# Attention feeding a routed MoE: other q and k loads and transposes, a separate load for the last queries' sums, expert weights loaded during attention

## The chip, the cores and the metric

One Trainium2 chip, one of its cores. The metric is the device time of one execution of the whole program in microseconds (us), the median of several executions. All profile times below are of one profiled execution.

## The reference, cut to what matters

The program chains three blocks on B=4 batches, H=8 heads, S=576 tokens, head size D=64 (N = 2304 tokens of width 512), all in float32:

```python
scores = scale * np.matmul(q, k.transpose(0, 1, 3, 2))          # attention, causal,
cum = np.cumsum(np.log(np.clip(f, 0.0001, 1.0)), axis=-1)       # with a decay from the forget gates f
scores = np.where(causal, -1e9, scores + cum[..., :, None] - cum[..., None, :])
attn = softmax(scores); x = matmul(attn, v)                     # -> (2304, 512)

e = argmax(x @ w_gate)                                          # MoE: 8 experts, top 1
y[mask_e] = gate_e * (relu(x[mask_e] @ w1[e]) @ w2[e])          # w1 512x1024, w2 1024x512

out = (silu(y @ w_gate2) * (y @ w_val)) @ w_out                 # GLU, width 1536
```

## The kernel before, in words

**Attention.** Work goes by pairs of heads: 16 pairs, four to a batch. A pair has five chunks of queries, `ic` 0 to 3 with 128 queries and (ic+1)·128 keys, and `ic` 4, the last 64 queries of both heads against all 576 keys, stacked into one 128-row product. For each pair:

- `load_qk` (L322) loads q and k with four DMAs each. Each partition gets 18 whole rows of 64 numbers (4608 bytes in a piece), and the two halves of a row go to two groups of 32 partitions by loading the rows twice, shifted. `qk_t` (L358) then turns 32x32 blocks on VectorE, writing with a step of 18 elements and reading 32 of every 64.
- `load_bc` (L335) broadcasts the pair's two rows of the running sums `cum` (scaled by -8) to all partitions, 576 columns a head, into the tile `bc`.
- On GpSimd, `dec_c` (L413) copies `bc` into `dec`, each head on its 64 partitions, in two copies, and adds the causal mask `future` to the last 64 columns. `qk_z` (L407) copies the last 64 queries into a block-diagonal tile `qz`, in two copies. `bc_m` (L423) writes the causal mask into each 128-column block of `bc`, once per chunk and head, after the chunk to its right has been used.
- `sc_mm` (L430) makes the scores in PSUM tiles of the tag `s` (4 buffers, two for each `ic`). `sc_max` and `sc_max4` (L451, L461) on VectorE add `bc` or `dec` and take the row's extreme. `sc_exp` (L471) exponentiates on ScalarE, `tr_mm` (L479) transposes on TensorE, `tr_ev` copies back, `av_mm` (L534) multiplies by v, `tok_mm` (L552) turns the result back to tokens and forms the gate's logits.

After each batch's last pair the routing runs: `route_a` to `route_g` on VectorE, `route_m` (L669) scales the rows of a chunk (on GpSimd for the first three batches, by the list `LAST_M` for the last), `route_w` (L687) scatters them by an indirect DMA on GpSimd to their expert's rows in DRAM, `xs`.

**What sets the order.** No engine reorders. `Plan` (L55) is a list scheduler that runs when the program is built: every step is added with an engine, a cost in ns, a priority (`PR`, plus the pair's number), dependences, buffers taken and released (`NB`), and for loads a DMA time. It simulates the engines and emits each engine's instructions in the order it finds. Where a cost or a DMA time in the plan is off, an instruction that waits stands in front of others on its engine. SyncE's DMA queue (SPq) carries all plain loads in that order.

**Pair 0** is loaded in another layout and transposed on TensorE (`first_load` to `first_e`), and its `bc` is made by a matmul from the sums in SBUF, not by a DMA (`bc_mm`, `bc_ev`).

**Bridge and MoE.** After the plan, the attention's memory is released. The pools `ring` (weights: four `raw` tiles, four `hl` tiles) and `mp` are opened on that memory. `w_load` (L908) loads a quarter of an expert's w1 (four DMAs of 128 KB) and of its w2 (one of 512 KB). At L1237 two quarters are loaded, `x_load(0)` loads expert 0's rows from `xs`, `w_split` (L926) splits the first quarter into a rounded part (ScalarE) and its remainder (VectorE), `offsets` (L1085) works out where each expert's tokens start, 24 (`NKEEP`) matmuls on constants keep TensorE going (L1245), then `x_turn` and `x_low` transpose and split the rows and `gemm1` begins. The MoE loop then runs over 8 experts with 8 chunks each. The GLU follows.

Of the kernel before, what the change touches and what calls it, by code (L numbers as in the profile page):

```python
# [20 lines left out]
P = 128  # L21
NEG = -8.0e9

PR = dict(
    ldq=-2.3,
# [5 lines left out]
    z=-0.6,  # L31
# [16 lines left out]
    zr=1.2,  # L48

# [89 lines left out]
def moe_kernel(ctx: ExitStack, tc: tile.TileContext, q, k, v, f, wgate, w1, w2, m2g, m2v, m2o, out):  # L139
# [56 lines left out]

    attn = ctx.enter_context(ExitStack())
# [25 lines left out]
    def pairwise(name, shape, fill=0.0):  # L223
        t = [one.tile(shape, F32, name=f"{name}{i}") for i in range(2)]
        return t

    v_sb = pairwise("v_sb", [P, NC, 2, D])
# [4 lines left out]
    p3 = pairwise("p3", [P, 2, 64])  # L232
    for i in range(2):
        nc.gpsimd.memset(qz[i], 0.0)
        nc.gpsimd.memset(v_sb[i][64:, NC - 1], 0.0)
# [78 lines left out]
    def load_v(p):  # L314
        b, hp = divmod(p, NP)
        for hh in range(2):
            nc.sync.dma_start(
                out=v_sb[p % 2][:, 0:4, hh], in_=v[b, 2 * hp + hh, 0:512].rearrange("(c p) d -> p c d", p=P)
            )
        nc.sync.dma_start(out=v_sb[p % 2][:64, 4], in_=v[b, 2 * hp : 2 * hp + 2, 512:576].rearrange("h p d -> p h d"))  # L320

    def load_qk(p, i):  # L322
# [3 lines left out]
        for hh in range(2):  # L326
            for dh in range(2):
                a = hh * 64 + dh * 32
                c = 32 - 32 * dh
                nc.sync.dma_start(  # L330
                    out=o.qk[i][a : a + 32, c : c + 18 * 64],
                    in_=(q, k)[i][b, 2 * hp + hh].rearrange("(c t) d -> c (t d)", t=18),
                )

    def load_bc(p):  # L335
        b, hp = divmod(p, NP)
        o = pairs[p]
# [1097 lines left out]
```

## Time and profile before

| | us |
|---|---|
| median of 3 runs | 978.03 |
| lowest, highest | 976.2, 982.95 |
| the profiled execution's own time | 977.45 |
| its span, first to last instruction | 975.7 |

| stage | from, to (us) | what ends it |
|---|---|---|
| attention, 16 pairs | 0 to 243 | last route steps |
| bridge | 243 to 266 | first `gemm1` matmul |
| MoE | 266 to 510 | |
| GLU | 510 to 976 | |

TensorE is busy for 903.8 us of the span (93%), VectorE 590.3, ScalarE 400.5, GpSimd 311.2. Engines are called PE, DVE, ACT and POOL in the rows; PEld is TensorE's weight load, SPq SyncE's DMA queue. A busy PE counts modelled ends of pipelined matmuls. "Idle before" a row, in brackets, is the time for which the engine stood idle, with what ended it. [...]

### The profile page before, as it was taken

To read this page: it belongs to the slowest core of one execution; us is meant where nothing else is said; L and a number is where in the kernel's file an instruction comes from. 1 tells how busy PE (TensorE), PEld (TensorE's weight loads), DVE (VectorE), ACT (ScalarE), POOL (GpSimd) and SP (SyncE) were. 2 spreads that over 40 slices of the span, in tenths; PEclk is the share of its full clock that TensorE was granted. 3 is DMA by queue.
4 is the path that set the end of the run, shared out by engine and by line. 5 is a ranking of instruction groups with operands and counts; after the bars stand their busy time and mean duration, and the time that the engine had idled before them with its cause. 6 is when DMAs were issued, how large, how long until landed. Compare 5 with 4: busy or idle time off the path is not lost. (4 is left out here: it accounts for less than half of the span.)

```text
span 975.7 us, 15236 instructions
## 1 busy us (share of the span) xinstructions
PE 903.8 (93%) x5046; PEld 739.0 (76%) x5048; DVE 590.3 (61%) x1409; ACT 400.5 (41%) x964; POOL 311.2 (32%) x435
## 2 busy tenths in 40 slices
PE   8988798998486999999979999999999999999995
PEld 4655455655286999999977888888888888888884
DVE  5666565675443666777872355755755756747653
ACT  5666466766333455555642522222322222222210
POOL 5335327361253000000112423423433334334334
PEclk8999899999687999999998999999999999999998
DMA  8965565620699977777632101201101111110013
GB/s 192 245 165 163 147 159 162 163 94 13 191 123 116 216 206 193 189 210 213 199 102 73 65 22 44 65 23 44 65 22 43 47 41 44 44 44 22 1 65 129
DMA packets 98562, 106.47 MB, mean 109 GB/s; under 512 B 29424, under 2 KB 80624, under 8 KB 98480
## 3 DMA queue, kind: packets, MB, share of 16 engines
q1 hardware_dynamic: 94864, 96.00, 38.9%
q0 software_dynamic: 3616, 9.46, 2.8%
q8 instruction: 41, 0.67, 0.3%
q14 instruction: 41, 0.34, 0.1%
HBM read 89.62 MB, written 15.81 MB: 108 GB/s over the span
## 5 line engine op out<-in xcount | busy, mean ns | idle before, releaser
L994 PE MATMUL h<-xhl,hl 128*128 128x320 f32 (+6 forms) x768 | 127.7, 317 | 24.0 <-ACT hl L934 12.1
L1361 PE MATMUL r<-hl,phl 128*128 128x512 f32 x594 | 146.4, 393 | 0.1
L994 PEld LDWEIGHTS h<-xhl,hl 128*128 128x128 f32 x768 | 118.2, 197 | 26.4 <-ACT hl L934 12.9
L1334 PE MATMUL v<-yh,hl 128*128 128x512 f32 (+1 forms) x440 | 134.8, 372 | 0.0
L1334 PE MATMUL g<-yh,hl 128*128 128x512 f32 (+1 forms) x440 | 134.3, 371 | 0.0
L1344 DVE TENSOR_TENSOR sg<-v,sg 128x512 f32<-128x512 f32 (+1 forms) x60 | 38.2, 636 | 158.7 <-PE v L1334 158.7
L1361 PEld LDWEIGHTS r<-hl,phl 128*128 128x128 f32 x594 | 110.8, 188 | 24.8 <-DVE acc L1366 0.5
L1366 DVE TENSOR_TENSOR acc<-r,acc 128x512 f32<-128x512 f32 x198 | 127.1, 683 | 3.9 <-PE r L1361 3.7
L1204 POOL TENSOR_TENSOR cs<-ca,cs 128x512 f32<-128x512 f32 x36 | 47.2, 1311 | 248.5 <-PE y L1013 146.2
L1349 POOL TENSOR_TENSOR phl<-sg,phl 128x512 fp32r<-128x512 f32 (+1 forms) x55 | 68.5, 1245 | 168.3 <-ACT phl L1346 168.3
L1013 PE MATMUL y<-hh,hl 128*128 128x320 f32 (+6 forms) x768 | 121.9, 309 | 0.0
L1013 PEld LDWEIGHTS y<-hh,hl 128*128 128x128 f32 x768 | 114.8, 192 | 0.0
L935 DVE TENSOR_TENSOR hl<-raw,hl 128x512 fp32r<-128x512 f32 x128 | 84.9, 708 | 42.0 <-ACT hl L934 33.1
L474 ACT ACTIVATE u<-u,mn 128x576 f32<-128x576 f32 (+2 forms) x144 | 83.7, 583 | 57.9 <-DVE mn L466 28.8
L1346 ACT ACTIVATE phl<-sg 128x512 fp32r<-128x512 f32 (+1 forms) x60 | 35.4, 591 | 166.8 <-DVE sg L1344 166.8
L456 DVE CUSTOM_DVE_ANT_0 u<-s,bc 128x512 f32<-128x512 f32 (+3 forms) x128 | 59.2, 486 | 64.2 <-PE s L444 30.3
L1334 PEld LDWEIGHTS g<-yh,hl 128*128 128x128 f32 x440 | 80.4, 188 | 15.3
L1334 PEld LDWEIGHTS v<-yh,hl 128*128 128x128 f32 x440 | 80.4, 188 | 15.1
L1343 ACT ACTIVATE sg<-g 128x512 f32<-128x512 f32 (+1 forms) x60 | 33.3, 555 | 140.9 <-PE g L1334 139.5
L934 ACT ACTIVATE hl<-raw 128x512 fp32r<-128x512 f32 x128 | 72.6, 621 | 37.8 <-DMA raw<-in_moe_w_dram 37.8
L1334 PE MATMUL v<-yl,hl 128*128 128x512 f32 (+1 forms) x220 | 81.2, 369 | 0.0
L1334 PE MATMUL g<-yl,hl 128*128 128x512 f32 (+1 forms) x220 | 81.2, 369 | 0.0
(193 smaller groups left out, 1317.9 us busy)
## 6 DMA issues: line engine op xcount, KB each, us to landing
raw<-in_moe_w_dram SPq DMA_DIRECT2D x128, 128.0 KB, 3.8
raw<-in_moe_w_dram SPq DMA_DIRECT2D x32, 512.0 KB, 4.5
qk<-in_q_dram SPq DMA_DIRECT2D x60, 144.0 KB, 4.3
qk<-in_k_dram SPq DMA_DIRECT2D x60, 144.0 KB, 5.1
bc<-cum_d SPq DMA_DIRECT2D x15, 576.0 KB, 6.2
xs<-zrow SPq DMA_DIRECT2D x8, 768.0 KB, 5.9
raw<-in_moe_w_gate_dram SPq DMA_DIRECT2D x12, 512.0 KB, 3.6
raw<-in_moe_w_val_dram SPq DMA_DIRECT2D x12, 512.0 KB, 3.5
```

What stands on the lines that cost most here:

```text
L456: nc.vector.tensor_tensor_reduce(out=st.U[:, :W], in0=st.ps[:, :W], in1=o.bc[:, hh, :W], op0=ALU.add, op1=ALU.min, scale=-0.125, scalar=3. ...
L474: nc.scalar.activation(out=st.U[:, :W], in_=st.U[:, :W], func=AF.Exp, bias=o.mn[:, x : x + 1], scale=-1.0, accum_out=o.sm[:, u : u + 1],)
L934: nc.scalar.activation(out=t[:, 0, j], in_=src[:, j], func=AF.Copy)
L935: nc.vector.tensor_tensor(out=t[:, 1, j], in0=src[:, j], in1=t[:, 0, j].bitcast(F32), op=ALU.subtract)
L994: nc.tensor.matmul(ps[:, :n], lhsT=w[:, a, c, f0 : f0 + P], rhs=xhl[e][:, b, c, :n], start=m == 0, stop=m == 3 * KC - 1)
L1013: nc.tensor.matmul(ys[e][c][:, : win(e)], lhsT=w[:, a, fc % 2, c * P : (c + 1) * P], rhs=t[:, b], start=fc == 0 and m == 0, stop=fc == NF ...
L1204: nc.gpsimd.tensor_tensor(out=s.bitcast(F32), in0=a.bitcast(F32), in1=s.bitcast(F32), op=ALU.add)
L1334: nc.tensor.matmul(pgv[fc, ti][y][:, :n], lhsT=w[:, a, y, c, :], rhs=(yh, yl)[b][:, c, t0 : t0 + n], start=m == 0, stop=m == 3 * KC - 1,)
L1344: nc.vector.tensor_tensor(out=sg[:, :n], in0=pv[:, :n], in1=sg[:, :n], op=ALU.mult)
L1349: en.tensor_tensor(out=t[:, 1, :n], in0=sg[:, :n], in1=t[:, 0, :n].bitcast(F32), op=ALU.subtract)
L1361: nc.tensor.matmul(ps, lhsT=t[:, a, x : x + P], rhs=w[:, b, :DM], start=m == 0, stop=m == 2)
L1366: nc.vector.tensor_tensor(out=o, in0=ps, in1=o, op=ALU.add)
```

## The change

- **q and k.** The loads take row t·32+c to partition c and cut each row into its two halves of 32 numbers: no byte is loaded twice, and each piece is 128 bytes. The transposes read and write whole rows of 576 without steps.
- **Sums.** `bc` covers only the first 512 columns. `dec` is loaded by two DMAs of its own (64 partitions each, 576 columns, three buffers); the two GpSimd copies are gone, and `dec_m` only adds the mask. For pair 0 `dec` comes from matmuls too.
- **Last queries.** `qz` is made by one multiplication with a 0/1 mask `own`, and waits for q's transpose alone.
- **Scores.** `ic` 0 shares the two PSUM tiles of `ic` 1.
- **Buffers and plan.** v gets three buffers; costs in the plan are changed; in the last batch the scatters no longer have an order among themselves in the plan, and `LAST_M` gives ScalarE one chunk in place of two.
- **Weights.** `ring` and a small pool `early` (for `offsets`) are opened before the attention's pools. The first two `w_load` and the first `w_split` become steps of the plan.
- `NKEEP` goes from 24 to 48.

```diff
 PR = dict(
+    ldd=-1.8,
...
+    w=0.0,
+    ws=0.0,
...
+    late = ctx.enter_context(ExitStack())
+    ring = late.enter_context(tc.tile_pool(name="ring", bufs=1))
+    early = late.enter_context(tc.tile_pool(name="early", bufs=1))
     attn = ctx.enter_context(ExitStack())
...
-    LAST_M = ["dve", "act", "dve", "act", "pool"]
-    NKEEP = 24
-    NB = dict(qk0=2, qk1=2, bc=3, qkt=2, dec=2, u=6, pt=2, s=4, t=2, o=2, v=2, x=2, xo=1, z=2)
+    LAST_M = ["dve", "dve", "act", "dve", "pool"]
+    NKEEP = 48
+    NB = dict(qk0=2, qk1=2, bc=3, qkt=2, dec=3, u=6, pt=2, s=4, t=2, o=2, v=3, x=2, xo=1, z=2)
...
                 nc.sync.dma_start(
-                    out=o.qk[i][a : a + 32, c : c + 18 * 64],
-                    in_=(q, k)[i][b, 2 * hp + hh].rearrange("(c t) d -> c (t d)", t=18),
+                    out=o.qk[i][a : a + 32, :S].rearrange("p (t d) -> p t d", d=32),
+                    in_=(q, k)[i][b, 2 * hp + hh].rearrange("(t c) d -> c t d", c=32)[:, :, dh * 32 : dh * 32 + 32],
                 )
...
-        nc.sync.dma_start(out=o.bc, in_=cum_d[None, h : h + 2, :].to_broadcast([P, 2, S]))
+        nc.sync.dma_start(out=o.bc, in_=cum_d[None, h : h + 2, :512].to_broadcast([P, 2, 512]))
+
+    def load_dec(p):
...
+        for x in range(2):
+            nc.sync.dma_start(
+                out=o.dec[x * 64 : x * 64 + 64], in_=cum_d[None, h + x, :].to_broadcast([64, S])
+            )
...
-        nc.vector.transpose(
-            out=o.t[:, i].rearrange("p (c t) -> p t c", t=18),
-            in_=o.qk[i][:, 32:].rearrange("p (t x) -> p t x", x=64)[:, :, 0:32],
-        )
+        nc.vector.transpose(out=o.t[:, i], in_=o.qk[i][:, :S])
...
-        for hh in range(2):
-            r = slice(hh * 64, hh * 64 + 64)
-            pcopy(qz[p % 2][r, hh * 64 : hh * 64 + 64], pairs[p].t[r, 0, 512:576])
+        nc.gpsimd.tensor_tensor(
+            out=qz[p % 2].rearrange("p (h i) -> p h i", h=2), in0=own,
+            in1=pairs[p].t[:, 0, None, 512:576].to_broadcast([P, 2, 64]), op=ALU.mult,
+        )
...
-        for hh in range(2):
-            r = slice(hh * 64, hh * 64 + 64)
-            pcopy(o.dec[r], o.bc[r, hh])
-        d = o.dec[:, 512:576]
+        d = pairs[p].dec[:, 512:576]
         nc.gpsimd.tensor_tensor(out=d, in0=d, in1=future, op=ALU.add)
...
+        for c, at in ((0, 256), (1, 0)) if ic == 1 else ((ic, 0),):
+            W = (c + 1) * P
...
-            lb = add("sp", 475, p + PR["bc"], partial(load_bc, p), [fs], acq=["bc"], data=1900)
+            lb = add("sp", 475, p + PR["bc"], partial(load_bc, p), [fs], acq=["bc"], data=1500)
+            ldc = add("sp", 900, p + PR["ldd"], partial(load_dec, p), [fs], acq=["dec"], data=800)
...
-        z = add("pool", 500, p + PR["z"], partial(qk_z, p), tt, acq=["z"])
-        dc = add("pool", 1560, p + PR["dc"], partial(dec_c, p), [lb], acq=["dec"])
+        z = add("pool", 420, p + PR["z"], partial(qk_z, p), tt[:1] if p else tt[4:5], acq=["z"])
+        dc = add("pool", 280, p + PR["dc"], partial(dec_m, p), [ldc])
...
-            c = 2 * c_f32(W) if ic == 4 else 1.5 * c_f32(W) + 200
+                c = {4: 1020, 3: 1060, 2: 840, 1: 960}[ic]
...
-                t = add("pe", (ic + 1) * 109, kk + PR["tr"] + 0.001 * hh, partial(tr_mm, p, hh, ic, st), [e], acq=["t"],
+                t = add("pe", (ic + 1) * 110 + 90, kk + PR["tr"] + 0.001 * hh, partial(tr_mm, p, hh, ic, st), [e], acq=["t"],
...
+    for qi in range(2):
+        l = add("sp", 2250, NPR - 3 + PR["w"] + qi, partial(w_load, 0, qi), data=4500)
+        if qi == 0:
+            d = l
+            for part in range(2):
+                for x in range(2):
+                    d = add("act", c_act(512), NPR - 1 + PR["ws"] + 0.1 * (2 * part + x), partial(w_hi, 0, 0, part, x), [l, d])
+                    d = add("dve", c_dve(512), NPR - 1 + PR["ws"] + 0.1 * (2 * part + x), partial(w_lo, 0, 0, part, x), [d])
     plan.run()
...
-    w_load(*qs[0])
-    w_load(*qs[1])
     x_load(0, 0)
-    w_split(0, 0, 0)
-    w_split(0, 0, 1)
     places = offsets()
```

## Rows read from the trace of the kernel before

**Rows 1.** Busy time by stage: PE, PEld, DVE, ACT, POOL, clock, DMA share, GB/s.
```profile
15.00:243.00 228.00, 201.73 (x1344) 128.00 (x1345) 144.37 (x542) 148.90 (x469) 95.70 (x230) 0.96 0.58 151
243.00:266.00 23.00, 8.37 (x29) 3.52 (x30) 10.48 (x55) 7.52 (x24) 5.96 (x6) 0.69 0.64 174
266.00:317.00 51.00, 38.86 (x201) 37.41 (x201) 21.60 (x47) 15.44 (x33) 20.68 (x20) 0.77 1.00 127
317.00:510.00 193.00, 190.28 (x1337) 189.56 (x1336) 139.81 (x298) 104.03 (x225) 8.41 (x6) 1.00 0.71 191
510.00:975.00 465.00, 451.79 (x2088) 373.75 (x2088) 266.83 (x429) 118.20 (x206) 172.10 (x140) 0.99 0.15 48
```

**Rows 2.** Line L466, the first DVE step of each pair: ns min/median/max, first to last start.
```profile
L466 DVE CUSTOM_DVE_ANT_0 u<-s,dec x16: 395/444/457, 14.5 to 223.1; 128x288 f32<-128x288 f32 x16
```

**Rows 3.** Timeline at 48 to 52 us: start, length, instruction, idle before it.
```profile
48.09 1.41 POOL L249 TENSOR_SCALAR dec<-bc 64x576 f32<-64x576 f32 x2 [5.14 <-DMA bc<-cum_d]
...
50.18 0.42 DVE L456 CUSTOM_DVE_ANT_0 u<-s,bc 128x256 f32<-128x256 f32 x1 [4.49 <-POOL bc L426]
...
51.84 0.55 PE L489 MATMUL pt<-ident,u 128*128 128x128 f32 x3 [2.60 <-ACT p L500]
```

**Rows 4.** Timeline at 103 and at 167 to 171 us.
```profile
103.63 0.24 POOL L249 TENSOR_SCALAR qz<-qkt 64x64 f32<-64x64 f32 x1 [4.73 <-DMA xs<-xo,slot_i]
103.93 2.29 PE L436 MATMUL s<-qkt,qz 128*128 128x288 f32 x4 [4.07 <-POOL qz L249]
...
167.28 0.67 POOL L249 TENSOR_SCALAR dec<-bc 64x576 f32<-64x576 f32 x1 [2.06 <-DMA xs<-xo,slot_i]
...
170.29 0.90 PE L489 MATMUL pt<-ident,u 128*128 128x128 f32 x3 [2.89 <-ACT p L500]
```

**Rows 5.** Busy time in two stretches of attention, columns as in rows 1.
```profile
100.00:120.00 20.00, 15.90 (x87) 9.08 (x89) 10.66 (x38) 9.74 (x31) 6.50 (x19) 0.83 0.40 121
160.00:180.00 20.00, 16.28 (x102) 10.26 (x101) 9.96 (x36) 12.46 (x37) 10.65 (x27) 0.91 0.66 175
```

**Rows 6.** Two DVE transposes: line L362 in attention, and L963 in the bridge's timeline.
```profile
L362 DVE STREAM_TRANSPOSE qkt<-qk x30: 1209/1252/1260, 13.4 to 210.8; 128x576 f32<-128x576 f32 x30
...
264.46 1.69 DVE L963 STREAM_TRANSPOSE xt<-xw 128x320 f32<-128x320 f32 x4 [2.17 <-DMA xw<-xs]
```

**Rows 7.** Groups by line, 0 to 260 us: count, busy us, mean ns, idle before.
```profile
L249 POOL TENSOR_SCALAR dec<-bc 64x576 f32<-64x576 f32 x32 | 21.3, 667 | 43.2 <-DMA bc<-cum_d 27.9 <-DVE mn L466 11.0 <-DMA xs<-xo,slot_i 2.1
```

**Rows 8.** DMA packets, MB and engine share in 6:7, 221:225 and 11:12 us.
```profile
q1 hardware_dynamic: 323, 0.01, 17.3%
...
q1 hardware_dynamic: 1200, 0.30, 32.5%
...
q1 hardware_dynamic: 87, 0.27, 106.5%
```

**Rows 9.** The bridge: timeline, and the five last scatters' time to landing.
```profile
247.53 1.82 SPq L913 DMA_DIRECT2D raw<-in_moe_w_dram  x4
...
250.44 0.98 POOL L690 DMA_INDIRECT xs<-xo,slot_i  x1 [0.30 <-issue]
...
DMA to landing us min/median/max: 2.8/3.3/8.8
...
259.28 1.82 SPq L949 DMA_DIRECT2D xw<-xs  x4
...
265.57 5.16 PE L994 MATMUL h<-xhl,hl 128*128 128x320 f32 x24 [11.30 <-issue]
```

**Rows 10.** The bridge: constant matmuls on PE, one weight split on ACT.
```profile
247.16 7.11 PE L1246 MATMUL y<-warm,ones 128*128 128x512 bf16 x22 [0.22 <-issue]
...
253.03 1.15 ACT L934 ACTIVATE hl<-raw 128x512 fp32r<-128x512 f32 x2 [5.57 <-DMA raw<-in_moe_w_dram]
```

**Rows 11.** Line L466 in DVE's timeline: the quickest pair.
```profile
116.74 0.43 DVE L466 CUSTOM_DVE_ANT_0 u<-s,dec 128x288 f32<-128x288 f32 x1
128.66 0.45 DVE L466 CUSTOM_DVE_ANT_0 u<-s,dec 128x288 f32<-128x288 f32 x1
```

More of the change, by code (lines that the diff above doesn't have):

```diff
@@ L221, in moe_kernel, with pairwise @@
     setup = []
[L223 to L227, printed above, removed]
+    def pairwise(name, shape, n=2):
+        return [one.tile(shape, F32, name=f"{name}{i}") for i in range(n)]
+    v_sb = pairwise("v_sb", [P, NC, 2, D], 3)
     xl = pairwise("xl", [P, NC, H, W2])
@@ L232, in moe_kernel @@
     p3 = pairwise("p3", [P, 2, 64])
+    setup_t = one.tile([B * H, 2, S], F32, name="setup_t")
+    own = one.tile([P, 2, 64], F32, name="own")
+    nc.gpsimd.memset(own, 0.0)
+    for x in range(2):
+        nc.gpsimd.memset(own[x * 64 : x * 64 + 64, x], 1.0)
+    for i in range(3):
+        nc.gpsimd.memset(v_sb[i][64:, NC - 1], 0.0)
     for i in range(2):
-        nc.gpsimd.memset(qz[i], 0.0)
-        nc.gpsimd.memset(v_sb[i][64:, NC - 1], 0.0)
         nc.gpsimd.memset(p3[i][64:], 0.0)
@@ L696, in route_w, with raw_tile, hl_tile, w_load @@
         scatters.append(i.ins)
+    def raw_tile():
+        return ring.tile([P, 1024], F32, tag="raw", name="raw", bufs=4)
+    def hl_tile():
+        return ring.tile([P, 2, 1024], F32R, tag="hl", name="hl", bufs=4)
+    raws = {}
+    def w_load(e, qi, at=None):
+        w1e, w2e = (w1[e], w2[e]) if at is None else (w1[bass.ds(at, 1)][0], w2[bass.ds(at, 1)][0])
+        a = raw_tile()
+        for blk in range(4):
+            nc.sync.dma_start(
+                out=a.rearrange("p (k f) -> p k f", k=KC)[blk * 32 : blk * 32 + 32],
+                in_=w1e[blk * P : (blk + 1) * P, qi * 256 : (qi + 1) * 256].rearrange("(k r) f -> r k f", r=32),
+            )
+        b = raw_tile()
+        nc.sync.dma_start(
+            out=b.rearrange("p (g d) -> p g d", g=2),
+            in_=w2e[qi * 256 : (qi + 1) * 256, :].rearrange("(g p) d -> p g d", p=P),
+        )
+        raws[e, qi] = (a, b)
+    hls = {}
+    def w_hi(e, qi, part, x):
+        if x == 0:
+            hls.setdefault((e, qi), []).append(hl_tile())
+        j = slice(x * 512, x * 512 + 512)
+        nc.scalar.activation(out=hls[e, qi][part][:, 0, j], in_=raws[e, qi][part][:, j], func=AF.Copy)
+    def w_lo(e, qi, part, x):
+        j = slice(x * 512, x * 512 + 512)
+        t = hls[e, qi][part]
+        nc.vector.tensor_tensor(
+            out=t[:, 1, j], in0=raws[e, qi][part][:, j], in1=t[:, 0, j].bitcast(F32), op=ALU.subtract
+        )
+    def w_split(e, qi, part):
+        for x in range(2):
+            w_hi(e, qi, part, x)
+            w_lo(e, qi, part, x)
     class St:
@@ L816, in moe_kernel @@
             mk = [
-                add("pool", 244, kk + PR["mk"], partial(bc_m, p, ic, hh), [lb, dc] + [mxs[hh, c] for c in range(ic + 1, 4)])
+                add("pool", 260, kk + PR["mk"], partial(bc_m, p, ic, hh), [lb] + [mxs[hh, c] for c in range(ic + 1, 4)])
                 for hh in range(2)
```

147 lines of the change are left out of this document (67 added, 80 removed).

## The prediction

> **What bounds the kernel now.** I read the busy time by stage first. The reader is to see there that the GLU and the MoE from 317 us on keep PE busy for 97 to 99% of the time at full clock [rows 1]: a step made earlier ahead of them can only shift them. The change works in the two stages before. Attention takes 228 us with PE busy for 88% of it, DVE 63%, ACT 65%, POOL 42%, and the DMA engines for 58%. The bridge, 23 us, leaves PE idle for nearly two thirds. Between them and the steady MoE lies a stretch, 266 to 317 us, where the DMA engines are full (1.00) and PE waits for weights.
>
> In attention the first DVE steps of the pairs spread over 208.6 us, so 15 intervals of 13.9 us [rows 2]. The timeline shows what lengthens some of them. At 48 us POOL stands 5.14 us at the copy into `dec` for the next pair, because that pair's `bc` has not landed; the masks of the current pair stand behind it, DVE waits 4.49 us, and PE loses 2.60 us [rows 3]. Twice POOL stands until a scatter has landed: at 103 us the second half of `qz` is behind it and PE loses 4.07 us, at 167 us a `dec` copy and again masks, and PE loses 2.89 us [rows 4]. The clock falls with these: the 20 us around the former were granted 0.83, around the latter 0.91 [rows 5]. As a clock of 0.5 for t takes t/2 of work away, that is 20 x 0.17 = 3.4 us and 20 x 0.09 = 1.8 us more.
>
> In the bridge the chain is: the last scatter is issued on POOL at 250.44; four of the five scatters land after some 3 us, but the slowest takes 8.8, and `x_load`, which must wait for all, goes out at 259.28, right when that one is down; 6.3 us later comes the first `gemm1` matmul [rows 9]. The weight loads, issued from 247.53 on, share the DMA engines with that scatter.
>
> **The change part by part.**
>
> *Bridge.* With two quarters (2 x 1 MB) loaded during attention, the five scatters are alone on the DMA engines. The last then lands after 2.8 to 3.3 us rather than 8.8 [rows 9]: 5.5 to 6.0 us less. `LAST_M` takes a chunk off ACT and lets POOL issue in the order in which chunks come ready, worth 0 to 1 us; I take none. But PE must also get through 48 constant matmuls before `gemm1`: 22 took 7.11 us and ended at 254.27 [rows 10], part of them at half clock; 24 more at the same 0.32 us each would be 7.8 us, at half that 3.9, so they end at 258.2 to 262.1; without them `gemm1` could start at 265.57 - 5.7 = 259.9. So the cost is 0 to 2.2 us, and near 0 as the clock has risen by then. The gain is 5.9, between 3.5 and 7. A higher clock in the first `gemm1` helps little: behind it the stretch to 317 us runs at the pace of the DMA engines [rows 1], and its loads are queued behind `x_load` as before, so that stretch is moved whole. The GLU too.
>
> *Splits in attention.* The first quarter's split is four ACT and four DVE steps: 1.15 us for two on ACT, so 2.3 us, and about as much on DVE, now in the last pair's plan, in front of steps that end the attention. ACT is idle 35% of the time, so it costs 0 to 2.3 us; I take 1. The wait for the weights is new on ACT: behind it stand the last pair's exponentials, but the ten DMAs are planned two pairs earlier. Their issue takes SPq some 5 us (1.82 us for four [rows 9]) ahead of the last v loads; a pair of 13.9 us covers that, and without the cover the last `av_mm` would wait as long.
>
> *POOL.* The two copies go, 2 x 0.667 us a pair [rows 7], and with them the place where POOL stands for `bc`. What comes in their stead is `dec_m`, which waits for its own DMA; behind it stand the masks again. But `dec` has three buffers, each free once the pair's first step has used it, so its load can be two pairs ahead. Of the three stalls I count back: 2.60 wholly; at 103 us half of 4.07 + 3.4, and at 167 us half of 2.89 + 1.8, since scatters still stand in POOL's queue. That is 2.6 + 3.7 + 2.3 = 8.6 us, between 0 (each stall moves to the next instruction in POOL's queue) and 14.8 (all go). `qz` as one step for two of 0.24 us [rows 4] changes little; that it no longer waits for k's transpose is in the same sum.
>
> *Transposes.* One takes 1.25 us for 576 columns. The nearest row without a step on the written side is the one in the bridge: four of 320 columns in 1.69 us, 0.42 each or 1.32 ns a column [rows 6]. That gives 0.76 for 576, 0.49 less, and 30 x 0.49 = 14.7 us of DVE time. DVE is not the bound (63%), but what stands behind a transpose on DVE feeds ACT and PE; the share that reaches the end lies between 0 and all. I take a third, 5 us, since PE, the busiest engine, was idle only 12%. [...]
>
> *DMA.* A 32-byte packet takes 0.173 x 16 us / 323 = 8.6 ns of one DMA engine (the window holds nearly nothing but `sel`), one of 256 bytes (v) 0.325 x 64 us / 1200 = 17.3 ns, one of 4608 bytes 1.065 x 16 us / 87, nearly 200 ns at the least as smaller ones are among the 87 [rows 8]. Before, q and k of a pair are 256 packets of 4608 bytes; by the 0.27 MB of that window in 17.0 us, 15.9 bytes a ns, they take 290 ns each and 256 x 290 / 16 = 4.6 us. After, they are 8 x 576 = 4608 packets of 128 bytes, between 8.6 and 17.3 ns each, so 2.5 to 5.0 us; on a line between the two, 12.3 ns and 3.5 us. `bc` and `dec` grow from 590 to 819 KB, at the same rate 2.3 to 3.2 us; v stays at 1152 x 17.3 / 16 = 1.2. In sum 7.9 us a pair for 8.1, of 13.9: no gain, no loss.
>
> *The rest.* Shared score tiles free two of ten takings of the four `s` buffers, v's third buffer takes waits off SPq, and more matmuls for pair 0's `dec` lengthen the start while two POOL copies there go. None has a row that prices it; with the new order as a whole I bound it by one stall of the size in rows 4 either way, -4 to +4 us, and take 0.
>
> **Sum.** 5.9 - 1 + 8.6 + 5 = 18.5 us. The profiled execution took 977.45, 1.75 over its span and 0.6 below the median, so 959.0. Extremes of the terms taken together: 3.5 - 2.3 + 0 + 0 - 4 = 2.8 us worse than before, and 7 + 14.8 + 14.7 + 4 = 40.5 better.
>
> **Rivals.**
>
> 1. *Only the bridge counts.* The stalls move to the next instruction behind the same scatters, and DVE's relief is hidden under PE at 88%. For it: two of three stalls end with a scatter [rows 4], and that is not changed. Against it: one of them is a wait for `bc` in a copy that no longer exists [rows 3]. Time: 977.45 - 5.9 + 1 = 972.5.
>
> 2. *PE becomes the pace of every pair.* The quickest pair took 11.92 us from first step to first step [rows 11]. If better costs in the plan and fewer waits brought all intervals to 12.2, attention would give 15 x 1.7 = 25.5 us, and the total is 977.45 - 25.5 - 5.9 + 1 = 947. Against it: routing steps come on top every fourth pair.
>
> 3. *Slower: small packets.* If a 128-byte packet cost 40 ns, q and k would need 4608 x 40 / 16 = 11.5 us and the pair 15.9, 2.0 more than 13.9. Over 15 pairs that is 30 us; less the bridge's 5.9 and plus 1, the time is 1003. It decides from (13.9 - 4.4) x 16 / 4608 = 33 ns on. Against it stand 17.3 ns for 256 bytes [rows 8]. [...]
>
> 4. *The loads are not ahead.* If the plan puts `w_load` so late that the weights meet the scatters again, the bridge stays and attention alone gives 13.6: 977.45 - 12.6 = 965.
>
> **How the numbers follow.** Forecast 0.62, at 959 with its own range of 951 to 967; rival 1, 0.16; rival 2, 0.12; rival 3, 0.04; rival 4, 0.06. A measurement of this kernel tells about 1%, 9.8 us, from no change: faster is below 968.2. The forecast, rivals 2 and 4 lie there, 0.80, and a quarter of rival 1's surroundings, 0.04: 0.84. Within 1% remains 0.12, slower 0.04. The range of 8 in 10 goes from 943, which takes in rival 2, to 972.
>
> **What would show it right or wrong.** In the changed profile the transposes should take about 0.8 us; no DMA of weights should be issued between attention and `x_load`; the last scatter should land after about 3 us, and `gemm1` start some 9.5 us after that scatter's issue rather than 15.1 [rows 9]; first steps of pairs should be about 13.0 us apart; POOL should have no `dec` copies, and fewer PE gaps of over 2 us should be left. The forecast is wrong if 128-byte packets take over 33 ns, if PE still has gaps of 3 us behind POOL, if the intervals fall to 12.2, or if the constant matmuls end after the rows have come.

## The result and the profile after

The changed kernel took 953.37 us, the median of 4 runs (950.29 to 959.41), beside 977.12 of the kernel before: a ratio of 0.976, with a 95% interval of 0.972 to 0.980. Measured a second time, beside the kernel before again, it had 964.22 against 982.24, 0.985 with 0.979 to 0.991. Both lie in the predicted range and on either side of the 959.0 forecast. The profiled execution is the quickest of the first four, 950.29 for 977.45 before, so its 27.2 us are more than the typical gain.

The busy time by stage of the changed kernel comes first: attention, bridge, the stretch of expert 0, the other experts, the GLU (columns as in [rows 1]; the clock is the granted share of TensorE's full one).

```profile
16.00:232.00 216.00, 196.80 (x1357) 125.34 (x1357) 140.37 (x559) 153.58 (x481) 77.91 (x188) 0.97 0.68 144
232.00:246.00 14.00, 13.40 (x51) 5.49 (x51) 6.21 (x39) 0.89 (x3) 4.16 (x4) 0.80 0.46 134
246.00:285.00 39.00, 30.97 (x180) 29.00 (x179) 17.89 (x41) 12.73 (x27) 20.55 (x20) 0.87 0.93 145
285.00:487.00 202.00, 194.41 (x1359) 192.87 (x1358) 143.21 (x305) 108.32 (x230) 8.38 (x6) 0.99 0.75 192
487.00:948.00 461.00, 451.07 (x2088) 372.74 (x2087) 266.90 (x429) 117.04 (x205) 172.34 (x140) 0.99 0.14 46
```

Beside [rows 1] the reader sees the bridge shrink from 23 to 14 us. The two stretches behind it have other borders there (266 to 317 and 317 to 510 us), so they are compared by exact borders. These are the starts of single instructions in the timelines: the matmul of `carry` that ends the attention, the `x_load` of expert 0, the first `gemm1` matmul, the first `gemm1` of expert 1, the first GLU matmul. All kernels are read by them, one profile each, in us:

| kernel | median | ratio to before (95%) | attention ends | `x_load` | first `gemm1` | expert 0 takes | expert 1 to GLU |
|---|---|---|---|---|---|---|---|
| before | 977.12 | | 246.33 | +12.95 | +6.29 | 45.7 | 202.2 |
| changed | 953.37 | 0.976 (0.972–0.980) | 232.44 | +6.83 | +6.37 | 39.4 | 201.7 |
| changed, again | 964.22 | 0.985 (0.979–0.991) | 236.06 | +6.82 | +6.23 | 46.5 | 202.3 |
| e1 weights back | 963.13 | 0.982 (0.977–0.988) | 228.82 | +10.77 | +8.18 | 45.9 | 203.8 |
| e2 24 constant matmuls | 963.79 | 0.984 (0.979–0.989) | 236.45 | +6.81 | +6.43 | 41.6 | 204.2 |
| e3 old q and k | 970.55 | 0.989 (0.982–0.996) | 240.72 | +6.82 | +6.34 | 48.9 | 202.6 |
| e4 mask order | 948.98 | 0.970 (0.965–0.975) | 217.63 | +6.90 | +6.18 | 49.0 | 204.5 |
| e5 weights late | 962.61 | 0.982 (0.977–0.987) | 230.01 | +6.85 | +6.15 | 46.4 | 204.8 |
| e6 POOL copies | 967.45 | 0.988 (0.983–0.994) | 238.61 | +6.82 | +6.29 | 45.5 | 205.3 |
| e7 old costs | 971.30 | 0.989 (0.985–0.993) | 241.45 | +6.90 | +6.30 | 49.1 | 205.7 |
| e8 order, late | 951.26 | 0.968 (0.963–0.972) | 223.27 | +6.85 | +6.23 | 54.2 | 201.6 |
| e9 perm late | 966.44 | 0.983 (0.979–0.987) | 236.61 | +6.82 | +6.33 | 28.2 | 225.6 |
| e10 order, perm | 951.71 | 0.969 (0.965–0.973) | 220.41 | +6.89 | +6.20 | 27.8 | 226.9 |
| e11 all three | 954.98 | 0.971 (0.967–0.975) | 220.89 | +6.85 | +6.28 | 31.0 | 227.4 |

Kernels measured side by side are e1 to e4, the repeat with e5 to e7, and e8 to e11; totals are compared within these groups. In the first and the last, e2 and e9 stand for the changed kernel, as their attention has its schedule. The totals expected of e1 to e4 were reckoned from 953.37, some 10 us below what the same schedule took there (963.79 in e2), so the differences count.

Of the 27.2 us between the two profiled executions, 13.9 come from the attention, 6.1 from the end of attention to `x_load`, 6.3 from expert 0 and 0.9 from the rest. The 6.3 are no effect of the change: the repeat took 46.5 us there, and over the ten kernels that leave that stretch as it was the time goes from 39.4 to 54.2. Attention spreads less: the changed one's schedule ran in four kernels (changed, its repeat, e2, e9) and ended at 232.44 to 236.61, mean 235.4. Against the one profile of before, a typical gain is 10.9 in attention and 6.1 in the bridge, 17 us of 977, which is between the two measured ratios.

The bridge, in the timeline of the changed kernel (answers to [rows 9, 10]):

```profile
232.44 0.17 PE L1147 MATMUL h<-carry,ones 128*128 128x8 bf16 x1 [1.06 <-DVE carry L672]
...
232.47 13.01 PE L1293 MATMUL y<-warm,ones 128*128 128x512 bf16 x48
...
236.09 0.98 POOL L714 DMA_INDIRECT xs<-xo,slot_i  x1 [0.30 <-DVE rk_m L1179]
...
239.27 1.84 SPq L1000 DMA_DIRECT2D xw<-xs  x4
...
245.63 4.38 PE L1045 MATMUL h<-xhl,hl 128*128 128x320 f32 x24 [0.16 <-ACT xhl L1019]
```

`x_load` goes out 3.2 us after the last scatter's issue (8.8 before), and `gemm1` starts 9.5 us after it (15.1 before). The 48 constant matmuls end at 245.48, 0.15 us ahead of `gemm1`, which waits for ACT and not for them. (The rows had landed by 244.52, when DVE began to transpose them.)

In attention the two PE gaps behind scatters have gone. The one behind `bc` at 50 us is larger, and a second one behind `bc` has come at 107 us. PE's gaps of over 2 us up to the last pair's end, 2.60, 4.07 and 2.89 before, are 4.35 and 5.41 now, 9.8 us for 9.6. The timeline of the changed kernel (answers to [rows 3, 4]):

```profile
44.08 0.45 SPq L347 DMA_DIRECT2D bc<-cum_d  x1
...
48.51 1.03 POOL L445 TENSOR_SCALAR_AFFINE_SELECT bc<-bc 128x128 f32<-128x128 f32 x4 [6.74 <-DMA bc<-cum_d]
49.33 0.29 DVE L480 CUSTOM_DVE_ANT_0 u<-s,bc 128x128 f32<-128x128 f32 x1 [4.83 <-POOL bc L445]
...
50.69 0.90 PE L513 MATMUL pt<-ident,u 128*128 128x128 f32 x3 [4.35 <-ACT p L524]
...
103.69 0.54 POOL L445 TENSOR_SCALAR_AFFINE_SELECT bc<-bc 128x128 f32<-128x128 f32 x2 [5.15 <-DMA bc<-cum_d]
105.90 0.29 DVE L480 CUSTOM_DVE_ANT_0 u<-s,bc 128x128 f32<-128x128 f32 x1 [5.91 <-POOL bc L445]
...
107.27 0.90 PE L513 MATMUL pt<-ident,u 128*128 128x128 f32 x3 [5.41 <-ACT p L524]
```

POOL now stands at a mask itself. In the order that the plan made, it is the first mask of pair 4, whose `bc` was issued on SPq at 44.08 and has landed when the mask starts at 48.51. Behind it stand the last two masks of pair 2, which is still in hand: pair 3 begins on DVE only at 50.43. What these two depend on, DVE's steps on the chunk to their right, had ended at 43.80, and yet they run only after the mask in front. DVE waits 4.83 us for one of these masks, then ACT and PE. At 103.69 it is the first mask of pair 8, ahead of the last two of pair 6. So the step in front belongs not to the next pair but to the one after it. The granted clock of the two stretches shows what follows the gaps:

```profile
41.00:61.00 20.00, 15.65 (x95) 9.68 (x95) 8.20 (x32) 10.33 (x34) 3.79 (x13) 0.83 0.94 199
98.00:118.00 20.00, 14.59 (x94) 8.80 (x92) 8.33 (x33) 10.35 (x33) 4.29 (x17) 0.83 0.71 140
50.70:57.50 6.80, 6.80 (x27) 3.23 (x29) 3.42 (x14) 3.56 (x11) 0.86 (x3) 0.56 0.92 202
```

In the 6.8 us behind the first gap (the third line) PE is busy all the time at a mean of 0.56 of its clock, so it does up to 3 us (6.8 x 0.44) less work than at full clock. In the 5.3 us ahead of the gap, from 41 to 46.3, the clock was 1.00.

By groups of the whole kernel (ns min/median/max, first to last start), the transposes fell from 1252 to 774 ns, and the first DVE steps of the 16 pairs are 12.95 us apart, (209.5 - 15.2) / 15, for 13.9 before [rows 2, 6]:

```profile
L388 DVE STREAM_TRANSPOSE qkt<-qk x30: 729/774/779, 13.4 to 193.4; 128x576 f32<-128x576 f32 x30
...
L490 DVE CUSTOM_DVE_ANT_0 u<-s,dec x16: 420/454/458, 15.2 to 209.5; 128x288 f32<-128x288 f32 x16
```

The packets of one us in which only k loads were issued, from the DMA view of 11.5 to 12.5 us:

```profile
q1 hardware_dynamic: 1098, 0.14, 85.0%
```

That is 0.85 x 16 us / 1098 = 12.4 ns for one packet of 128 bytes (0.14 MB in 1098). And one thing is far from where the prediction had it: the early weights. SPq, ACT and DVE in the timeline of 51 to 75 us:

```profile
51.99 2.01 SPq L735 DMA_DIRECT2D raw<-in_moe_w_dram  x4
54.05 0.43 SPq L740 DMA_DIRECT2D raw<-in_moe_w_dram  x1
64.28 0.63 ACT L752 ACTIVATE hl<-raw 128x512 fp32r<-128x512 f32 x1
...
66.27 2.02 SPq L735 DMA_DIRECT2D raw<-in_moe_w_dram  x4
```

Both quarters are loaded and the first split in pairs 3 to 5, not in the last pairs: in the plan these loads depend on nothing, so they go out as soon as SPq has no step of higher priority ready.

### The profile page after: what moved, and what is told of

Its sections match the earlier page's. It is cut to its first block, busy times and chain, and to the rows that moved or that the text cites. A ratio compares the mean times of both kernels' runs of the same rounds, so it can differ in the third digit from the quotient of the medians.

```text
span 948.5 us, 15310 instructions
## 1 busy us (share of the span) xinstructions
PE 901.1 (95%) x5080; PEld 733.2 (77%) x5080; DVE 581.8 (61%) x1410; ACT 399.7 (42%) x958; POOL 291.1 (31%) x389
## 5 line engine op out<-in xcount | busy, mean ns | idle before, releaser
L1045 PE MATMUL h<-xhl,hl 128*128 128x320 f32 (+6 forms) x768 | 123.5, 309 | 8.6 <-issue 6.8
L1045 PEld LDWEIGHTS h<-xhl,hl 128*128 128x128 f32 x768 | 113.8, 190 | 11.4 <-issue 7.6
L498 ACT ACTIVATE u<-u,mn 128x384 f32<-128x384 f32 (+4 forms) x144 | 83.8, 584 | 45.6 <-DVE mn L480 33.4
L480 DVE CUSTOM_DVE_ANT_0 u<-s,bc 128x128 f32<-128x128 f32 (+3 forms) x128 | 59.8, 484 | 55.0 <-POOL bc L445 28.8
L1381 PEld LDWEIGHTS v<-yh,hl 128*128 128x128 f32 x440 | 80.3, 188 | 15.1
```

The costliest lines, as they stand in the source:

```text
L480: nc.vector.tensor_tensor_reduce(out=st.U[:, :W], in0=st.ps[:, at : at + W], in1=o.bc[:, hh, :W], op0=ALU.add, op1=ALU.min, scale=-0.125, ...
L498: nc.scalar.activation(out=st.U[:, :W], in_=st.U[:, :W], func=AF.Exp, bias=o.mn[:, x : x + 1], scale=-1.0, accum_out=o.sm[:, u : u + 1],)
L1045: nc.tensor.matmul(ps[:, :n], lhsT=w[:, a, c, f0 : f0 + P], rhs=xhl[e][:, b, c, :n], start=m == 0, stop=m == 3 * KC - 1)
L1381: nc.tensor.matmul(pgv[fc, ti][y][:, :n], lhsT=w[:, a, y, c, :], rhs=(yh, yl)[b][:, c, t0 : t0 + n], start=m == 0, stop=m == 3 * KC - 1,)
```

## The experiments

**The weights taken out of attention (e1).** All weights are loaded after the attention again, as before the change; the rest of the change stays.

```diff
-    for qi in range(2):
-        l = add("sp", 2250, NPR - 3 + PR["w"] + qi, partial(w_load, 0, qi), data=4500)
-        ...
+    w_load(*qs[0])
+    w_load(*qs[1])
     x_load(0, 0)
+    w_split(0, 0, 0)
+    w_split(0, 0, 1)
```

> The changed kernel with its weight part undone: ring opened after attention, the first two quarters loaded and the first split made in the bridge, as before (the 48 constant matmuls stay). My theory, that this part is worth 5.9 us in the bridge and costs 1 in attention: about 958, with the last scatter landing after some 8 us again and x_load some 13 us after the last carry step rather than 7. Rival A, that the quicker first expert (39.4 us after the change, 45.7 before) also comes from this part: 961 to 965. Rival B, that the weight loads, which the plan issued at 52 and 66 us into full DMA queues, hold attention up: it ends earlier, and the total is 955 or less.

The bridge's timeline in e1:

```profile
232.47 0.98 POOL L711 DMA_INDIRECT xs<-xo,slot_i  x1 [0.30 <-issue]
232.62 3.07 SPq L732 DMA_DIRECT2D raw<-in_moe_w_dram  x4
...
239.59 1.82 SPq L991 DMA_DIRECT2D xw<-xs  x4
...
247.77 5.67 PE L1036 MATMUL h<-xhl,hl 128*128 128x320 f32 x24 [7.09 <-issue]
```

From the last scatter's issue to `x_load` are 7.1 us (8.8 before the change, 3.2 with the weights ahead), and from there to `gemm1` 8.2 for 6.4. Together 5.8 us of the bridge hang on the early weights, the size predicted, though a third of it (1.8) lies behind `x_load` and not in the scatter. Attention, however, ends at 228.82, some 6 us before the mean of the changed kernel: of PE's two gaps the one at 50 us is still there (3.98 us), the one at 107 us is not. What the bridge gains by the early loads, attention gives back; in the total e1 can't be told from the changed kernel.

**Fewer constant matmuls (e2).** `NKEEP` is 24 again.

```diff
-    NKEEP = 48
+    NKEEP = 24
```

> The changed kernel with 24 constant matmuls instead of 48. My theory: the clock falls before gemm1, its first 24 matmuls take some 1 us longer, and that is hidden because the stretch behind it waits for weights: 953, within 2 us. Rival: the kept clock is what made the first expert quicker (39.4 us for 45.7): 956 to 960, and the stretch from gemm1 to the second expert is back at some 45 us. Rival 2: the 48 ended after the rows had come (245.5 us), so fewer of them start gemm1 earlier: 952.

```profile
237.29 6.28 PE L1293 MATMUL y<-warm,ones 128*128 128x512 bf16 x22 [0.22 <-issue]
...
249.69 5.59 PE L1045 MATMUL h<-xhl,hl 128*128 128x320 f32 x24 [6.12 <-ACT xhl L1019]
```

In e2's bridge PE stands 6.12 us before `gemm1`, and the first 24 matmuls take 5.59 us for 4.38: 1.2 us in the place itself. Of that nothing is seen in the total (0.984, between the two measurements of the changed kernel). So the doubled count costs nothing, and what it is worth is below what can be told.

**The old loads and transposes of q and k (e3).** `load_qk` and `qk_t` as before the change, with `WQ` of 1184.

```diff
-                    out=o.qk[i][a : a + 32, :S].rearrange("p (t d) -> p t d", d=32),
-                    in_=(q, k)[i][b, 2 * hp + hh].rearrange("(t c) d -> c t d", c=32)[:, :, dh * 32 : dh * 32 + 32],
+                    out=o.qk[i][a : a + 32, 32 - 32 * dh : 32 - 32 * dh + 18 * 64],
+                    in_=(q, k)[i][b, 2 * hp + hh].rearrange("(c t) d -> c (t d)", t=18),
...
-        nc.vector.transpose(out=o.t[:, i], in_=o.qk[i][:, :S])
+        nc.vector.transpose(
+            out=o.t[:, i].rearrange("p (c t) -> p t c", t=18),
+            in_=o.qk[i][:, 32:].rearrange("p (t x) -> p t x", x=64)[:, :, 0:32],
+        )
```

> The changed kernel with the old loads of q and k and the stepped transposes; plan costs and so the order of every engine are unchanged. A transpose goes from 0.77 to 1.25 us. My theory, that a third of the VectorE time comes through: 14.4 / 3 = 5 us, so about 958. Rival A, VectorE is hidden: 953 within 2. Rival B, all of it comes through: 967. Rival C, the small packets cost more than the transposes win: under 951.

The group of transposes in e3, from the lines of 0 to 260 us (busy us, mean ns):

```profile
L388 DVE STREAM_TRANSPOSE qkt<-qk 128x576 f32<-128x576 f32 x30 | 36.7, 1251 | 3.8 <-DMA qk<-in_q_dram 2.7 <-DMA qk<-in_k_dram 0.9 <-PE s L469 0.2
```

DVE has 14 us more of transposes, and attention ends at 240.72, 5.3 later than the changed kernel's mean (4.1 to 8.3 by its single readings). That is about the third that the prediction took. The total is 6.8 us over e2's beside it, though their intervals overlap. The order of every engine is the changed kernel's here, but loads and transposes are undone together, so the price is that of both.

**The order of masks and `dec` (e4).** POOL's step on the next pair's `dec` and the next pair's masks are made to depend, in the plan, on the current pair's last masks. POOL then does the current pair's masks first. The same steps are computed. As the plan works out all queues anew, the others change as well: 53 of POOL's 196 steps stand in another order, 26 of PE's 325, 29 of DVE's 364, 26 of ACT's 325 and 2 of SPq's 88.

```diff
+    mk = []
...
-        dc = add("pool", 280, p + PR["dc"], partial(dec_m, p), [ldc])
+        dc = add("pool", 280, p + PR["dc"], partial(dec_m, p), [ldc] + mk)
+        last_mk = mk
...
-                add("pool", 260, kk + PR["mk"], partial(bc_m, p, ic, hh), [lb] + [mxs[hh, c] for c in range(ic + 1, 4)])
+                add("pool", 260, kk + PR["mk"], partial(bc_m, p, ic, hh), [lb] + last_mk + [mxs[hh, c] for c in range(ic + 1, 4)])
```

> The changed kernel with two added dependences in the plan: the first masks of a pair and the mask of dec come after the last masks of the pair before, so that nothing that waits for a pair's loads stands on GpSimd in front of the pair before. My theory, that the two TensorE gaps left (4.35 and 5.41 us, each with 6.8 us at half clock behind it, 16.6 us in all) come from that order: both gone, and 8 to 14 us less, 939 to 945. Rival: bc is late in any case, so the wait moves to VectorE's first step on bc and the time stays within 3 of 953.

POOL's largest wait in e4's attention (us in total, times, longest), the pairs' first steps, and the busy time in the two stretches:

```profile
POOL bc L445 <- DVE mn L480: 102.1, 68, 6.0
```

```profile
L490 DVE CUSTOM_DVE_ANT_0 u<-s,dec x16: 396/458/459, 14.5 to 193.8; 128x288 f32<-128x288 f32 x16
```

```profile
41.00:61.00 20.00, 19.92 (x136) 12.57 (x136) 13.49 (x53) 16.95 (x55) 4.97 (x18) 1.00 0.97 203
98.00:118.00 20.00, 20.00 (x153) 13.53 (x153) 13.12 (x51) 15.84 (x51) 5.94 (x20) 1.00 0.93 175
```

In the changed kernel POOL waited 43.1 us for `bc` in 11 places and 26.4 for `dec` in 11:

```profile
POOL bc L445 <- DMA bc<-cum_d: 43.1, 11, 6.7
POOL dec L440 <- DMA dec<-cum_d: 26.4, 11, 5.0
```

Neither line is among e4's waits: POOL waits for DVE's minima, and no masks stand behind a load of `bc` or `dec`. PE is busy all the time in the two stretches, at full clock. Attention ends at 217.63 although the DMA engines are as full (0.97). The pairs are 11.95 us apart, (193.8 - 14.5) / 15. The total is 14.8 us below e2's beside it. By the plan's own reckoning its steps end at 209.6 us in the changed kernel and at 211.2 in e4: it rates the better order as the worse one. In it pair 4's `bc` lands at 40.4 us, just before pair 2's last masks are due (41.1), so nothing seems lost by going first; on the chip it has landed at 48.4, 3.9 us after DVE ran out of work. What part the small shifts on the other engines have in the gain was not tried.

**The changed kernel again.** The same kernel, measured beside e5 to e7.

```diff
+# (a comment)
```

> The changed kernel once more, with nothing changed but a comment, to see how much its stages differ from run to run. Attention and bridge: the carry matmul within 1.5 us of 232.4, and the bridge within 0.5 us of the former. The stretch from gemm1 to the second expert took 39.4 us in the first profile, but 41.6 to 49.0 in three kernels with the same MoE; if it is chance, it lies anywhere from 39 to 49 here. If it stays at 39.4, the three kernels changed it.

It took 964.22, 0.985 of before. Its attention has both gaps again (3.6 us at 51 and 5.4 us at 108) and ends 3.6 us later than in the first profile, more than the 1.5 expected; the bridge agrees, and expert 0 takes 7.1 us more. It gives the measure for all that follows: 4 us in attention and some 15 in expert 0 mean nothing in a single profile.

**The early weights held back (e5).** The loads of the two quarters wait in the plan for `av_mm` of pairs 11 and 12.

```diff
-        l = add("sp", 2250, NPR - 3 + PR["w"] + qi, partial(w_load, 0, qi), data=4500)
+        l = add("sp", 2250, NPR - 3 + PR["w"] + qi, partial(w_load, 0, qi), [avs[11 + qi]], data=4500)
```

> The changed kernel with the two weight loads held in the plan until the twelfth and thirteenth pair are through, so that they go out after 160 us. My theory, that at 52 and 66 us they stand in front of other loads in full queues and make the gap at 107 us: that gap goes or shrinks to under 2 us, the gap at 51 us stays, attention ends 3 to 8 us earlier, the bridge keeps its 6.8 us, total 4 us under the changed kernel. Rival: the small packets fill the queues anyway; the gap at 107 us stays and the time is the same within 2.

```profile
181.10 3.09 SPq L735 DMA_DIRECT2D raw<-in_moe_w_dram  x4
...
192.44 2.16 SPq L735 DMA_DIRECT2D raw<-in_moe_w_dram  x4
```

The stretch that had the gap at 107 us (columns as in [rows 1]):

```profile
98.00:118.00 20.00, 18.91 (x136) 12.80 (x135) 12.65 (x54) 15.37 (x50) 7.01 (x22) 1.00 0.66 158
```

The loads go out at 181 and 192 us, the bridge stays as short (+6.85), and attention ends at 230.01, 5.4 before the mean. As expected, the gap at 107 us goes (PE's longest there is 0.87 us, at full clock) and the one at 50 us stays (3.27). In e1 it is the same, while all six profiles with the changed order and the loads at 52 and 66 us (changed, repeat, e2, e3, e6, e9) have a gap of 5.4 to 7.6 us between 107 and 112 us. So the early loads cost this one gap. The total gains 1.6 us on the repeat's, within the error.

**POOL's old copies as mere load (e6).** Two copies a pair of the old size, on tiles of their own that nobody waits for, ahead of `dec_m`.

```diff
+        for hh in range(2):
+            nc.gpsimd.tensor_scalar(out=junk[hh * 64 : hh * 64 + 64], in0=jsrc[hh * 64 : hh * 64 + 64],
+                                    scalar1=1.0, scalar2=1.0, op0=ALU.mult, op1=ALU.mult)
         d = pairs[p].dec[:, 512:576]
```

> The changed kernel with two copies of 64x576 added on GpSimd ahead of each mask of dec, from a constant tile into one that nobody reads: the work of the old copies is there again, their wait for bc is not; the plan does not know of them, so the order is the same. My theory, that what the copies cost was their wait and place more than their time: attention ends 1 to 4 us later. Rival A, GpSimd at 42% hides them: within 1 us. Rival B, all 16 x 1.33 = 21 us: 10 or more later.

Attention ends at 238.61, 3.2 after the mean (2.0 to 6.2), and the total is 3.2 us over the repeat's, within the error. POOL's time itself is worth little, by one profile; its place in the queue, by e4, is worth more.

**The old costs in the plan (e7).** The estimates of the score matmuls, of the transposes of p and of `av_mm` are those of the kernel before; the instructions are the changed kernel's, in the order that these estimates give.

```diff
-                c = {4: 1020, 3: 1060, 2: 840, 1: 960}[ic]
+                c = 2 * c_f32(W) if ic == 4 else 1.5 * c_f32(W) + 200 + (1.5 * c_f32(P) + 200) * (ic == 1)
...
-                    t = add("pe", 4 * 110 + 90 if y == 0 else 200, ...
+                    t = add("pe", 4 * 109 if y == 0 else 109, ...
```

> The changed kernel with TensorE's old costs in the plan (scores, transposes, products with v), so only the order changes. The prediction gave the new order as a whole nothing, within 4 us either way: attention ends within 4 us of the changed kernel's. Rival: the costs are what brings the gain that the transposes don't: attention ends 5 us later or more.

The larger of two gaps in e7 that answer to those at 50 and 107 us (the other has 3.57 us, at 83):

```profile
49.75 0.54 POOL L445 TENSOR_SCALAR_AFFINE_SELECT bc<-bc 128x128 f32<-128x128 f32 x2 [6.71 <-DMA bc<-cum_d]
...
53.50 0.69 PE L513 MATMUL pt<-ident,u 128*128 128x128 f32 x2 [5.80 <-ACT p L524]
```

Attention ends at 241.45, 6.1 after the mean (4.8 to 9.0), and the total is 7.1 over the repeat's, with intervals that overlap (0.985 to 0.993 and 0.979 to 0.991). The estimates alone, by which the plan orders the queues, are worth about as much as the transposes, as far as one profile tells.

**Both orders mended (e8).** e4's and e5's edits together.

```diff
+        dc = add("pool", 280, p + PR["dc"], partial(dec_m, p), [ldc] + mk)
...
+        l = add("sp", 2250, NPR - 3 + PR["w"] + qi, partial(w_load, 0, qi), [avs[11 + qi]], data=4500)
```

> The changed kernel with two edits: POOL's step on the next pair's dec stands behind the current pair's masks in the plan, and the two early weight quarters are issued only when av_mm of pairs 11 and 12 are planned. If the two gains are of different places (POOL's order of masks and bc; DMA queues shared with weights at 52 to 80 us), attention ends at about 213 to 217 us and the total is 940 to 948. If the late weights only helped through the same stalls, attention ends at 217 to 221, as with the mask order alone, and the total is 945 to 952.

Attention ends at 223.27, later than in e4 and than either expectation had it, and the total, 0.968 of before, is e4's 0.970 within the error. Once the masks no longer stand behind a DMA, holding the weights back gains nothing.

**The perm stores moved (e9).** The 20 indirect stores of `perm_d`, 4 bytes a row, and its load go from behind the bridge, where they ran beside expert 0, to step 49 of the MoE.

```diff
-    perm_store()
     engs = (mybir.EngineType.Activation, mybir.EngineType.DVE)
...
+        if g == CONV2[1]:
+            perm_store()
```

> The changed kernel with the 20 indirect stores of perm_d and its load moved from the bridge to step 49 of the MoE; nothing else. If these scatters of 4-byte pieces hold up the weight loads of expert 0, the time from the first gemm1 of expert 0 to the first of expert 1, 39.4 and 46.5 us in two profiles of the changed kernel, falls to 30 to 35, and the total to 945 to 955 (ratio near 0.97). If it is the loads themselves that are too late there (two quarters ahead only), the time stays at 39 to 46 and the total at 957 to 965.

The packets and the loads of weights (KB each, median us from issue to landing) in e9 at 250 to 290 us, where the stores used to be, and then at 432 to 472, where they are now:

```profile
q1 hardware_dynamic: 11227, 9.33, 92.8%
...
raw<-in_moe_w_dram SPq DMA_DIRECT2D x24, 128.0 KB, 4.9
```

```profile
q1 hardware_dynamic: 3549, 4.44, 83.4%
...
raw<-in_moe_w_dram SPq DMA_DIRECT2D x14, 128.0 KB, 11.5
...
perm_d<-tok_id,pos_i POOLq DMA_INDIRECT x20, 13.1
```

The repeat of the changed kernel, which has the stores at 250 to 290 us and none at 432 to 472, shows the reverse in the same two windows:

```profile
raw<-in_moe_w_dram SPq DMA_DIRECT2D x14, 128.0 KB, 11.2
...
raw<-in_moe_w_dram SPq DMA_DIRECT2D x24, 128.0 KB, 4.1
```

So wherever the stores are, the loads of 128 KB land after 11.2 to 11.5 us, and after 4.1 to 4.9 without them. In e9, per KB, a plain packet took 0.928 x 16 x 40 us / 9.33 MB = 64 ns without and 0.834 x 16 x 40 / 4.44 = 120 ns beside them. Busy time by stage, and the timeline of the place, show the gain and how it is given back:

```profile
250.00:278.00 28.00, 27.48 (x181) 26.42 (x181) 19.28 (x43) 13.92 (x31) 0.00 (x0) 1.00 0.94 241
278.00:430.00 152.00, 152.00 (x1030) 152.00 (x1029) 106.69 (x239) 81.24 (x174) 0.00 (x0) 1.00 0.75 200
430.00:490.00 60.00, 38.86 (x269) 37.81 (x268) 28.06 (x51) 20.34 (x45) 29.10 (x25) 0.84 0.77 107
```

```profile
463.50 1.15 ACT L752 ACTIVATE hl<-raw 128x512 fp32r<-128x512 f32 x2 [10.14 <-DMA raw<-in_moe_w_dram]
464.18 3.23 PE L1045 MATMUL h<-xhl,hl 128*128 128x256 f32 x12 [7.76 <-ACT hl L752]
```

Expert 0 falls to 28.2 us, with PE busy at full clock: the loads themselves were not too late, the stores held them up. But 430 to 490 us now has the gaps, and expert 1 to GLU rises from 202 to 225.6. The total is that of the changed kernel. My expectation of 945 to 955 missed that at step 49, too, loads two quarters ahead are no cover against the 20 stores.

**Masks and perm stores (e10), and all three (e11).** e4's edit with e9's, then with e5's as well.

```diff
+        dc = add("pool", 280, p + PR["dc"], partial(dec_m, p), [ldc] + mk)
...
+        if g == CONV2[1]:
+            perm_store()
```

> The changed kernel with POOL's step on dec behind the current pair's masks and with the perm stores at step 49. The two work in different stages, so the gains add if both theories hold: attention ends at 216 to 221 us, expert 0 takes 30 to 35, total 930 to 940 (ratio near 0.955). If the perm stores do not matter, 945 to 952.

> All three edits: the order of dec and masks, the early weights held back to pairs 11 and 12, the perm stores at step 49. If all three add: attention ends at 213 to 217, expert 0 in 30 to 35 us, total 926 to 936. If holding the weights back is worth nothing once the order of masks is mended, the same as with the two others, 930 to 940.

Side by side e9 took 966.44 and e10 951.71, and no run of the one is within 10 us of the other's: 14.7 us for the order that e4's edit makes, and the attention ends 16.2 us earlier. The totals of 930 to 940 and 926 to 936 were missed, as the moved stores give back in the MoE what expert 0 gains. e4's edit is the one that counts in the total: over the four kernels with it attention ends at 217.6 to 223.3, mean 220.6, for 235.4 without. e11 shows once more that late weights add nothing. The kernels with e4's edit have ratios of 0.968 to 0.971, below both measurements of the changed kernel (the first of these, 0.972 to 0.980, just overlaps), and of them e4 is the smallest edit: 948.98, interval 0.965 to 0.975. The perm stores in the GLU, where the DMA engines are at 0.14, were not tried.

## Why the prediction was right, and which steps of it were not

*Bridge, +5.9: right in size and reason.* 6.1 us up to `x_load`, which goes out 3.2 us after the last scatter's issue for 8.8; e1 puts 5.8 us of delay back when weights are loaded there, 3.9 of it ahead of `x_load`. The constant matmuls cost 0, as taken: by the letter of the prediction's test they "end after the rows have come" (245.48 for 244.52), but `gemm1` waits for the rows' transposes, and with half as many it starts no earlier (e2: 6.43 us after `x_load`, for 6.37 and 6.23). That the stretch behind is "moved whole" held on the average only: it spreads by 15 us from kernel to kernel, and 6.3 us of the first profile's gain are that spread.

*Splits and early loads, -1: the wrong place and too small.* The failed step is "the ten DMAs are planned two pairs earlier": they went out at 52 and 66 us. The two kernels without loads there (e1, e5) end attention at 228.8 and 230.0 rather than 235.4, so they cost some 6 us: the gap at 107 us, which both lack. The gap at 50 us is not theirs, as it begins before the first load is issued. Whether they make the other one by taking DMA time or by the order that the plan then gives is not settled; with the masks in order the same edit (e8, e11) gains nothing.

*POOL, +8.6: the step that failed.* I counted the stall at 48 us back "wholly", as the copy that stood there is gone. But what stood behind the copy was what mattered: in the new order the first mask of the same pair waits for the same `bc` in the same place, for 6.74 us. The prediction reads the copy at 48 us as the next pair's; it was pair 4's already, with pair 2's masks behind it. By the prediction's own test ("if PE still has gaps of 3 us behind POOL") this term is refuted: 4.35 and 5.41 us are there, as much in all as the old ones. The prediction named the mechanism, "each stall moves to the next instruction in POOL's queue", but priced it as the lower bound instead of looking at what the new queue holds. e4's edit shows its price, 14.7 us (e10 against e9) and 14.8 (e4 against e2). The sum is also a little high by itself: at 103 us it counts 3.4 us for half clock, but 2.5 us of that stretch (101.4 to 103.9) PE was idle.

*Transposes, +5: right in size.* 774 ns for 760 predicted, and 5.3 us at the end of attention by e3, loads included. That 1.34 ns a column (774 / 576) meets the bridge's 1.32 is in part luck, as that row is of four that overlap: each takes 470 to 512 ns, all four together 1.69 us. The changed kernel has single ones of 256 columns as well:

```profile
L1014 DVE STREAM_TRANSPOSE xt<-xw 128x256 f32<-128x256 f32 x4 | 1.7, 432 | 0.0
```

From 256 to 576 columns a column costs (774 - 432) / 320 = 1.07 ns, and by these two figures some 160 ns (432 - 256 x 1.07) come on top of each transpose.

*DMA, 0: right.* 12.4 ns for a 128-byte packet, 12.3 taken, and far from the 33 ns of rival 3. The engines' share in attention rose from 0.58 to 0.68, with the 2 MB of weights in it; with the old loads (e3) POOL's waits for `bc` are as long, 44.4 us in total and 6.6 the longest.

*The rest, 0 within 4: outside its bound, as far as one profile tells.* Undoing TensorE's estimates in the plan alone costs 6.1 us (e7). POOL's time without its waits is 3.2 (e6), which I had not separated from the stalls. The shared score tiles, v's third buffer, the new `qz` and `LAST_M` were not undone one by one.

The sum in attention, 12.6 predicted and 10.9 on the average, was right by luck, through errors of opposite sign: POOL's stalls gave no net gain and the early loads cost more, while the plan's new costs, which I had put at nothing, gave some 6. The single undoings (5.3, 6.1, 3.2, less 6) come to 8.6 and need not add.

Of the rivals, the first (only the bridge, 972.5) fell with attention's gain, the third with the packets' 12.4 ns, and the fourth with the bridge's gain; weights came too early, not too late. The second, PE's pace of 12.2 us a pair and 947, did not come with this change but does with e4: 11.95 us a pair, 948.98.

## What to carry to other kernels

When a step that waits for a DMA is taken out of an in-order queue, look at what the queue will then hold: if another step waits for the same transfer in the same place, the stall stays (here 5.14 us at the copy before and 6.74 at the mask after), and what counts is which steps stand behind it whose data are there already. Make the steps that the current tile needs go ahead of the first step of a later tile, by a dependency in the plan (14.7 us here, e10 against e9). And profile the changed kernel twice before a stage's gain is believed: here one stage varied by 15 us, more than half of the whole gain.

## What the runs showed of the hardware that was not expected

The 20 indirect stores of 4-byte rows held up the plain loads that shared the DMA engines with them: they more than doubled the landing of 128 KB loads, from 4.9 to 11.5 us in e9 and from 4.1 to 11.2 in the repeat, and packets took 120 ns a KB for 64, while the engines were counted 0.83 busy. They cost about 18 us of expert 0 (46.5 in the repeat, 28.2 in e9; 39.4 to 54.2 with them over all kernels, 27.8 to 31.0 without) and some 24 where they were moved to. A 128-byte packet of q and k at 12.4 ns carries 10.3 bytes a ns, for the 15.9 of the large ones in the prediction. By what the 4-byte stores held up the other loads no run here shows.

The granted clock went with the gaps on PE: the 4.35 and 5.41 us gaps of the changed kernel lie in stretches granted 0.83, with 0.56 in the 6.8 us behind the first, and the same stretches without gaps in e4 were granted 1.00. The first gap so cost up to 3 us more than its own length.
